# One weight through GpSimd's DMA queue, the next one held until the first copies of x are made, and a new split of the buffers

## The chip, the cores and the metric

The kernel runs on one core of one Trainium2 chip. The time is the device time of one execution in microseconds (us). The runs of the kernel before lie within 0.73 to 0.97 us in each of the four measurements of it (266.71 to 267.44 us in the first; 266.78 to 267.67, 266.73 to 267.50 and 266.60 to 267.57 in the others), that is 0.3 to 0.4% of 267, so everything here is near the resolution of the measurement: times are given as medians of several runs, with ratios and their 95% intervals, and the argument rests mainly on traces, where a single instruction can be placed to 0.01 us.

## The reference, cut to what matters

The input x has 2048 rows of 512. Two branches work on it and a gate mixes them:

```python
def _A_ref(x, wq, wk, wv, wo, beta):          # 32 heads of 16, 4 segments of 512 rows
    q, k, v = x @ wq, x @ wk, x @ wv          # ... split into heads and segments
    for s in range(4):
        # softmax attention inside the segment, plus a read of the memory M, z
        # that the segments before have left;  then M, z += phi(k)^T v, sum phi(k)
        ...
    return o @ wo
def _B_ref(x, W_gate, W_up, W_down):          # 512 -> 1792 -> 512
    return (relu(x @ W_gate) * (x @ W_up)) @ W_down
g = sigmoid((x * gate_w).sum(-1))
return g * a + (1 - g) * b
```

Each of wq, wk and wv is 512 x 512 bfloat16, 512 KB. The first segment of x is 512 KB as well. Nothing can be computed before x and wq are in, and K's projection needs wk.

## The kernel before: the parts that the change and the argument touch

The kernel is a list of operations with keys and estimated costs. A small scheduler inside it orders them for each engine when the program is built; on the chip the order is fixed. The start of the program is this (cuts marked with `...`):

```python
for _ in range(28):                            # warm-up of TensorE, on a tile of ones
    nc.tensor.matmul(g_dummy.t[:, 0:P], lhsT=zero[:, 0:P], rhs=zero[:, 0:P], start=True, stop=True)
...
for i in range(2):                             # i: column half of x, h: row half
    for eng, q, h in (("SP", nc.sync, 0), ("ACT", nc.scalar, 1)):
        ...  q.dma_start(out=xn[0].t[...], in_=x[...])          # 128 KB of x
    if i == 0:
        ...  q.dma_start(out=wq_sb[:, 0, cs], in_=A_wq[0:P, cs])  # wq chunk 0, 64 KB on SP, 64 KB on ACT
    else:
        ...  # wq chunk 1 (128 KB) on SP, chunks 2 and 3 (256 KB) on ACT
lw["wk"] = loadw("wk", wk_sb, A_wk, 0, D, 1)   # 512 KB, on SP
lw["wv"] = loadw("wv", wv_sb, A_wv, 0, D, 1)
...
first_x(0, None); first_x(1, None)             # TensorE transposes x, VectorE and ScalarE copy it to xT
for ci in range(NC):                           # q0.0 to q0.3: four matmuls of 512 columns each
    ...  nc.tensor.matmul(qS.t[:, c, :], lhsT=wq_sb[:, ci, ...], rhs=xT[0].t[:, ci, :], ...)
    if ci < 2: first_x(ci + 2, o_q0)
```

Then come K's projection (`wk_sb`, first seen as `G<-xT,wk_sb`), V's, and the long body: attention units (scores `S<-QT,K`, exponentials `E<-S`, masks, "PV" `G<-E,Vp`), mixed with the dense matmuls of the other branch. Buffers that the change touches:

```python
K2p = pool("K2", 6, [P, 8, 2, 64])
Ep = pool("E", 7, [P, 4, L])                   # the exponentials, until PV has read them
rgp = pool("rg", 3, [P, L]); osp = pool("os", 2, [P, D])
```

## Time and profile before

| | before |
|---|---|
| median of 4 runs | 266.94 us (266.71 to 267.44) |
| span of the profiled run | 265.7 us |
| TensorE busy | 256.3 us, 96% of the span |
| granted TensorE clock | 1.0 |
| first matmul of K's projection | 9.78 us |

The first lines are from the page of the kernel before: busy time by engine, and the head of the chain of work that ended last.

```profile
PE 256.3 (96%) x2795; PEld 114.5 (43%) x2832; DVE 182.5 (69%) x404; ACT 195.3 (73%) x191; POOL 188.4 (71%) x467
...
PE 95%; issue 2%; DMA 2%; SPq 0%; DVE 0%; DVEq 0%
```

TensorE is the bottleneck and has hardly a gap. What the chain has besides TensorE is 2% of DMA, and in order of time that is one piece at the start: 4.63 us from 2.27 us on, of a copy of wq. So the head is the place to look. This is TensorE's timeline there, in the kernel before (start, duration in us, engine, line, operation, count, and in brackets the idle time before it and what ended it):

```profile
1.11 3.13 PE L292 MATMUL G<-os 128*128 128x128 bf16 x28 [1.11 <-DVE mcole L269]
4.07 0.62 PE L390 MATMUL G<-ident,xn 128*128 128x128 bf16 x8
4.93 1.02 PE L411 MATMUL S<-xT,wq_sb 128*128 128x512 bf16 x4 [0.25 <-DVE xT L398]
6.34 0.48 PE L390 MATMUL G<-ident,xn 128*128 128x128 bf16 x4 [0.39 <-DMA xn<-in_A_x_dram]
6.96 1.04 PE L411 MATMUL S<-xT,wq_sb 128*128 128x512 bf16 x4
7.83 0.39 PE L390 MATMUL G<-ident,xn 128*128 128x128 bf16 x4
8.05 1.89 PE L411 MATMUL S<-xT,wq_sb 128*128 128x512 bf16 x7
9.78 2.75 PE L249 MATMUL G<-xT,wk_sb 128*128 128x512 bf16 x12
```

Read it as: 28 warm-up matmuls, transposes of x (`G<-ident,xn`), q0.0, a wait for the second pieces of x, transposes, q0.1, transposes, q0.2 and q0.3 (one record of eight is missing), then K. Four matmuls of 512 columns take 1.02 us when each starts 0.215 us after the one before. That number is used throughout below: **how long q0.0 takes tells the rate at which TensorE was running at that moment.**

The last piece is the page's list of DMA issues (median us from issue to landing):

```profile
wk_sb<-in_A_wk_dram SPq DMA_DIRECT2D x1, 512.0 KB, 5.9
xn<-in_A_x_dram ACTq DMA_DIRECT2D x2, 128.0 KB, 3.8
xn<-in_A_x_dram SPq DMA_DIRECT2D x2, 128.0 KB, 3.6
wq_sb<-in_A_wq_dram ACTq DMA_DIRECT2D x1, 256.0 KB, 5.0
wq_sb<-in_A_wq_dram SPq DMA_DIRECT2D x1, 128.0 KB, 4.6
```

wk was issued at 3.78 us and landed at 3.78 + 5.9 = 9.7 us, just when q0 was done.

### The profile page before, as it was taken

How to read it: one execution, taken by the hardware profiler on the slowest of the kernel's cores; microseconds unless marked ns; L12 is line 12 of the kernel's file. 1: busy time of each engine (PE TensorE's matmuls, PEld its weight loads, DVE VectorE, ACT ScalarE, POOL GpSimd, SP SyncE). 2: the span in 40 equal slices, each digit the busy share in tenths (PEclk: the TensorE clock that was granted, in tenths of full speed). 3: DMA queues.
4: the chain of work that ended last, by engine and by line, in shares of the span. 5: the costliest groups of instructions: out<-in, count | busy, mean ns of one | idle time of the engine just before them, and what ended most of it. 6: DMA issues, size and time to landing. Idle time of an engine off the chain costs nothing.

```text
span 265.7 us, 7041 instructions
## 1 busy us (share of the span) xinstructions
PE 256.3 (96%) x2795; PEld 114.5 (43%) x2832; DVE 182.5 (69%) x404; ACT 195.3 (73%) x191; POOL 188.4 (71%) x467
## 2 busy tenths in 40 slices
PE   7999999999999999999999999999999999999995
PEld 6434444444444444444444434344443444444444
DVE  1397888888975185998888837688985725466611
ACT  3498999899886658899896667898788566777010
POOL 8268888888559688798648988887878866537000
PEclk9999999999999999999999999999999999999999
DMA  6995991016310000000660010000000010000011
GB/s 171 309 268 145 333 241 25 2 38 78 103 23 23 22 20 22 0 2 0 131 109 3 23 42 21 2 0 2 0 2 4 0 42 20 23 2 0 2 41 39
DMA packets 27585, 15.54 MB, mean 58 GB/s; under 512 B 13600, under 2 KB 27552, under 8 KB 27552
## 3 DMA queue, kind: packets, MB, share of 16 engines
q1 hardware_dynamic: 26592, 14.50, 23.2%
q10 hardware_dynamic: 960, 0.59, 0.7%
q8 instruction: 22, 0.36, 0.6%
q14 instruction: 11, 0.09, 0.1%
HBM read 9.84 MB, written 2.10 MB: 45 GB/s over the span
## 4 chain that ended last, share of the span: by engine, by line
PE 95%; issue 2%; DMA 2%; SPq 0%; DVE 0%; DVEq 0%
PE G L249 74%; PE S L740 9%; PE G L852 7%; PE G L247 2%; DMA wq_sb<-in_A_wq_dram 2%; PE S L411 1%; PE G L613 1%; PE G L787 0%; SPq L317 0%; DVE os L702 0%; SPq L325 0%; PE G L390 0%; DVEq L702 0%
## 5 line engine op out<-in xcount | busy, mean ns | idle before, releaser
L754 ACT ACTIVATE E<-S 128x2048 bf16<-128x2048 f32 x72 | 135.1, 1876 | 32.1 <-PE S L740 29.4
L762 POOL TENSOR_SCALAR_AFFINE_SELECT E<-E 64x256 bf16<-64x256 bf16 x256 | 116.2, 454 | 39.2 <-ACT E L754 25.4
L249 PE MATMUL G<-xT,wu_sb 128*128 128x512 bf16 x210 | 57.1, 380 | 0.4 <-issue 0.2
L249 PE MATMUL G<-xT,wg_sb 128*128 128x512 bf16 x207 | 56.3, 380 | 1.1 <-issue 0.8
L665 DVE TENSOR_TENSOR hT<-G,rg 128x512 bf16<-128x512 f32 x56 | 38.2, 683 | 20.0 <-ACT rg L661 10.9
L249 PE MATMUL G<-wd_sb,hT 128*128 128x512 bf16 (+1 forms) x215 | 49.7, 366 | 1.3 <-issue 1.1
L887 DVE STREAM_TRANSPOSE T<-G 128x512 f32<-128x512 f32 x44 | 30.3, 702 | 13.0 <-PE G L852 8.2
L661 ACT ACTIVATE rg<-G 128x512 bf16<-128x512 f32 x56 | 32.7, 597 | 5.6 <-PE G L249 5.3
L249 PEld LDWEIGHTS <-wu_sb 128*128 128x128 bf16 x218 | 19.9, 98 | 24.8 <-issue 3.0
L249 PEld LDWEIGHTS <-hT 128*128 128x128 bf16 x226 | 20.5, 98 | 22.7 <-issue 3.0
L249 PEld LDWEIGHTS <-wg_sb 128*128 128x128 bf16 x218 | 19.4, 98 | 24.6 <-issue 4.1
L740 PE MATMUL S<-QT,K 32*128 32x192 bf16 (+7 forms) x512 | 28.6, 287 | 0.5
L740 PEld LDWEIGHTS <-K 32*128 32x128 bf16 x512 | 8.3, 92 | 30.2 <-issue 29.7
L702 DVE TENSOR_SCALAR os<-G,ngcol 128x512 bf16<-128x512 f32 (+1 forms) x8 | 5.5, 683 | 21.1 <-PE G L249 21.0
L852 PE MATMUL G<-E,Vp 64*32 64x128 bf16 (+7 forms) x512 | 19.0, 284 | 0.4 <-issue 0.4
L852 PE MATMUL G<-E,VS 64*32 64x128 bf16 (+7 forms) x512 | 18.4, 284 | 0.0
L599 POOL COPY VS<-Vp 64x256 bf16<-64x256 bf16 x32 | 12.9, 404 | 7.5 <-DVE Vp L517 6.0
L704 ACT ACTIVATE os<-G,ngcol 128x512 bf16<-128x512 f32 x9 | 6.2, 687 | 15.9 <-PE G L249 15.8
L249 PE MATMUL G<-wo_sb,oT 128*128 128x512 bf16 (+1 forms) x66 | 17.0, 367 | 0.3 <-issue 0.3
L907 DVE TENSOR_TENSOR O<-T,sm 128x256 bf16<-128x256 f32 x32 | 16.0, 529 | 0.3
L249 PE MATMUL G<-xT,wk_sb 128*128 128x512 bf16 x60 | 15.8, 380 | 0.3 <-issue 0.2
L481 POOL COPY R<-rcol 32x4 f32<-32x4 f32 x64 | 13.6, 212 | 3.0
(96 smaller groups left out, 295.5 us busy)
## 6 DMA issues: line engine op xcount, KB each, us to landing
out_dram<-os SPq DMA_DIRECT2D x15, 128.0 KB, 1.7
wd_sb<-in_B_W_down_dram SPq DMA_DIRECT2D x1, 1792.0 KB, 13.9
xn<-in_A_x_dram SPq DMA_DIRECT2D x3, 512.0 KB, 4.9
wg_sb<-in_B_W_gate_dram SPq DMA_DIRECT2D x2, 512.0 KB, 5.3
wu_sb<-in_B_W_up_dram SPq DMA_DIRECT2D x2, 512.0 KB, 6.6
wg_sb<-in_B_W_gate_dram SPq DMA_DIRECT2D x3, 256.0 KB, 6.7
wu_sb<-in_B_W_up_dram SPq DMA_DIRECT2D x3, 256.0 KB, 6.4
wk_sb<-in_A_wk_dram SPq DMA_DIRECT2D x1, 512.0 KB, 5.9
```

The lines of the kernel that those rows point to most:

```text
L249: nc.tensor.matmul(out_ap, lhsT=lhsT, rhs=rhs, start=start, stop=stop)
L481: nc.gpsimd.tensor_copy(R[s][32 * j:32 * j + 32, k, :], rcol[32 * k:32 * k + 32, cols])
L599: nc.gpsimd.tensor_copy(VS[s].t[64 * r:64 * r + 64, t, 0:H // 2 * HP].rearrange("p (h v) -> p h v", v=HP)[:, :, 0:DH], src[:, :, r, 0:DH])
L661: nc.scalar.activation(rg.t[:], g.t[:], ACT.Relu)
L665: nc.vector.tensor_tensor(h.t[:], u.t[:], rg.t[:], ALU.mult)
L704: nc.scalar.activation(ob.t[:, cs], g.t[:, 0:W], ACT.Copy, scale=ngcol[:, tt:tt + 1])
L740: nc.tensor.matmul(sp.t[:, j, off:off + w], lhsT=K2[s, cc].t[rows, kb, :, :].rearrange("p r k -> p (r k)"), rhs=QT[s, cc].t[rows, L - w:L] ...
L754: nc.scalar.activation(eb_.t[:], sp.t[:], ACT.Exp, scale=SCALE)
L762: nc.gpsimd.affine_select(out=v, in_=v, compare_op=ALU.is_ge, fill=0.0, base=0, pattern=[[0, 4], [1, 64]], channel_multiplier=-1)
L852: nc.tensor.matmul(gs[r].t[32 * j:32 * j + 32, L - w:L], lhsT=v, rhs=src.t[rows, j, off:off + w], start=(kb == 0), stop=(kb == 7), tile_po ...
L887: nc.vector.transpose(T.t[:].rearrange("p b e -> p (b e)"), g.t[:])
L907: nc.vector.tensor_tensor(O.t[:, :, r, :], T.t[:, :, 0:DH], sm.t[:, r, :, None].to_broadcast([P, 16, DH]), ALU.mult)
```

## The change

The intent: let x alone use SP's and ACT's queues, bring wq through GpSimd's queue at the same time, keep wk from competing with both until the first copy of x has been made, and use the space of some buffers for an eighth E. The hold on wk is a trick: VectorE writes one element of wk's tile after its first copies of x, so the load of wk must wait for that write. The diff, cut to its core:

```diff
-    K2p = pool("K2", 6, ...)
+    K2p = pool("K2", 5, ...)
-    Ep = pool("E", 7, [P, 4, L])
+    Ep = pool("E", 8, [P, 4, L])
-    rgp = pool("rg", 3, [P, L])
-    osp = pool("os", 2, [P, D])
+    osp = rgp = pool("os", 4, [P, D])
...
-        if i == 0:                     # wq on SP and ACT, between and after the pieces of x
-            ... (14 lines)
+    for n, (c0, c1) in enumerate(((0, 1), (1, 2), (2, 4))):
+        def f(e, c0=c0, c1=c1):
+            nc.gpsimd.dma_start(out=wq_sb[:, c0:c1, :], in_=A_wq[c0 * P:c1 * P, :].rearrange("(c p) n -> p c n", p=P))
+        o = op(f"wq{c0}", {"POOL": 1.0}, f, key=-110 + 15 * n, cls=0, land=131072 * (c1 - c0) / GBs)
...
     lw["wk"] = loadw("wk", wk_sb, A_wk, 0, D, 1)
+    o_wk0 = op("wk0", {"DVE": 0.08}, lambda e: nc.vector.memset(wk_sb[0:1, 0, 0:1], 0.0), key=-490, cls=0)
+    lw["wk"].deps.append((o_wk0, None))
...
+    o_wk0.deps.append((xc0[0][0], None))
...
-        (den and the memory update mz in one operation, with two PSUM buffers at once)
+        (mz an operation of its own, right behind den)
```

The rest of the diff makes the scheduler keep a valid order (the loads of later x segments are ordered behind wd, an operation may not start before its buffers have been given out).

More of the change, by code (lines that the diff above doesn't have):

```diff
@@ L59, in __init__, with op @@
         self.ops = []
-    def op(self, name, engs, emit, deps=(), key=0.0, cls=1, mode=None, alloc=(), uses=(), land=0.0, flex=False):
+    def op(self, name, engs, emit, deps=(), key=0.0, cls=1, mode=None, alloc=(), uses=(), land=0.0, flex=""):
         o = Op()
@@ L97, in run @@
                     t = max(free[e], o.ready)
-                    ok = True
+                    ok = all(b.idx is not None for b in o.uses[len(o.alloc):])
                     need = {}
@@ L119, in pk @@
                             k += -20.0 if mode == "R" else 4.0
-                        elif o.mode == "D" and mode == "C" and not o.flex:
+                        elif o.mode == "D" and mode == "C" and "C" not in o.flex:
                             k += 3.0
@@ L134, in run @@
             if e == "PE":
-                o.ran = "C" if o.flex and mode == "C" else o.mode
+                o.ran = mode if mode in o.flex else o.mode
                 if o.ran != mode:
@@ L213 @@
     hTp = pool("hT", 22, [P, L])
-    QTp, KTp, K2p = pool("QT", 6, [P, L]), pool("KT", 3, [P, L]), pool("K2", 6, [P, 8, 2, 64])
+    QTp, KTp, K2p = pool("QT", 6, [P, L]), pool("KT", 3, [P, L]), pool("K2", 5, [P, 8, 2, 64])
     pqp = pool("pq", 4, [P, L])
@@ L320 @@
                              uses=[] if (i, h) == (0, 0) else [xn[0]])
-        if i == 0:
-            for eng, q, h in (("SP", nc.sync, 0), ("ACT", nc.scalar, 1)):
-                def f(e, h=h, q=q):
-                    cs = slice(256 * h, 256 * h + 256)
-                    q.dma_start(out=wq_sb[:, 0, cs], in_=A_wq[0:P, cs])
-                lwq.setdefault(0, []).append(load(f"wq0{h}", f, 65536, -299.5, eng=eng))
-        else:
-            for c0, c1, eng, q in ((1, 2, "SP", nc.sync), (2, 4, "ACT", nc.scalar)):
-                def f(e, c0=c0, c1=c1, q=q):
-                    q.dma_start(out=wq_sb[:, c0:c1, :], in_=A_wq[c0 * P:c1 * P, :].rearrange("(c p) n -> p c n", p=P))
-                o = load(f"wq{c0}", f, 131072 * (c1 - c0), -298, eng=eng)
-                for ci in range(c0, c1):
-                    lwq[ci] = [o]
+    for n, (c0, c1) in enumerate(((0, 1), (1, 2), (2, 4))):
+        def f(e, c0=c0, c1=c1):
+            nc.gpsimd.dma_start(out=wq_sb[:, c0:c1, :], in_=A_wq[c0 * P:c1 * P, :].rearrange("(c p) n -> p c n", p=P))
+        o = op(f"wq{c0}", {"POOL": 1.0}, f, key=-110 + 15 * n, cls=0, land=131072 * (c1 - c0) / GBs)
+        for ci in range(c0, c1):
+            lwq[ci] = [o]
+    o_vones.deps.append((lwq[3][0], -1e9))
     def loadw(name, tile_, ap, c0, c1, key, eng="SP"):
@@ L422 @@
             lx[s] = xload(s, 10 + 60 * s)
+            for o in lx[s]:
+                o.deps.append((lwd, -1e9))
         xr[s] = [lx[s][0]]
@@ L509, in f @@
                     mm(g.t[:], lhs(ci), rhs(ci), ci == 0, ci == NC - 1)
-            prev = op(f"{name}/{i}", {"PE": 2 * MM}, f, deps=[(prev, 0.0)] if i else deps, key=dkey(2), mode="D", flex=True,
+            prev = op(f"{name}/{i}", {"PE": 2 * MM}, f, deps=[(prev, 0.0)] if i else deps, key=dkey(2), mode="D", flex="C",
                       alloc=[] if i else alloc, uses=uses + (alloc if i else []))
@@ L688, in dn @@
                           deps=[lwd, (prev, 0.0) if prev else None] + gate + [o_h[s, fb] for fb in range(p0, p1)],
-                          key=dkey((p1 - p0) / halves), mode="D", flex=True, alloc=[g] if p0 == 0 else [],
+                          key=dkey((p1 - p0) / halves), mode="D", flex="C", alloc=[g] if p0 == 0 else [],
                           uses=([] if p0 == 0 else [g]) + [hT[s, fb] for fb in range(p0, p1)])
@@ L697, in dn @@
                               deps=[lwo, (prev, 0.0)] + [o_oT[s, c] for c in (2 * i, 2 * i + 1)],
-                              key=dkey(2 / halves), mode="D", flex=True, uses=[g] + [oT[s, c] for c in (2 * i, 2 * i + 1)])
+                              key=dkey(2 / halves), mode="D", flex="C", uses=[g] + [oT[s, c] for c in (2 * i, 2 * i + 1)])
             def f(e, g=g, cs=cs):
@@ L788, in f @@
                                  start=True, stop=True, tile_position=(0, 32 * c))
-            if s < NSEG - 1:
-                mz_mm(s, gm)
-        gm, mds, mus = None, [], []
-        if s < NSEG - 1:
-            gm, mds, mus = Buf(G), mz_deps(s), [pK[s], Vp[s]]
-        a = op(f"den{s}", {"PE": MM + (0.5 if gm else 0.0)}, f,
-               deps=[o_pq[s, c] for c in range(NC)] + [o_m2[s - 1, c] for c in range(NC)] + mds,
-               key=k0, mode="C", alloc=[g] + ([gm] if gm else []), uses=[pq[s, c] for c in range(NC)] + mus)
-        rec_of[s, "den"] = a
-        if gm:
-            gate_mz.append((s, a, gm, k0))
+        mds = mz_deps(s) if s < NSEG - 1 else []
+        a = op(f"den{s}", {"PE": MM}, f,
+               deps=[o_pq[s, c] for c in range(NC)] + [o_m2[s - 1, c] for c in range(NC)] + mds,
+               key=k0, mode="C", alloc=[g], uses=[pq[s, c] for c in range(NC)])
+        rec_of[s, "den"] = rec_of[s, "mz"] = a
+        if mds:
+            gm = Buf(G)
+            rec_of[s, "mz"] = am = op(f"mz{s}", {"PE": 0.5}, lambda e: mz_mm(s, gm), deps=[(a, 0.0)], key=k0 - 20, mode="C",
+                                      alloc=[gm], uses=[pK[s], Vp[s]])
+            gate_mz.append((s, am, gm, k0))
         T = Buf(Tp)
@@ L866, in rest @@
             a = op(f"rec{s}{c}", {"PE": MM}, f, deps=[o_pq[s, c], o_m2[s - 1, c], (prev_pv, 0.0)],
-                   key=k0 + 3.6 * PU / 5, mode="D", flex=True, alloc=[g], uses=[pq[s, c]])
+                   key=k0 + 3.6 * PU / 5, mode="D", flex="C", alloc=[g], uses=[pq[s, c]])
             recs.append((a, g))
```

## The prediction

> **What bounds the kernel now.** TensorE: the page gives it 96% busy over a span of 265.7 us at granted clock 1.0, and the chain of waits that ended last is 95% TensorE, 2% DMA. By stretches, TensorE idles only 4.0 us between 30 and 250 us, in pieces of about 0.2 us[...], and 3.6 us at the tail. So only the head is left for a different order of loads.
>
> The head, from the timeline: x's first halves are transposed at 4.07 us, q0.0 runs 4.93 to 5.95, the second x pieces release the next transposes at 6.34, q0.1 starts at 6.96 on the landing of wq's second chunk (in the chain, a 4.63 us DMA ending at 6.90), q0.2 at 8.05, and K's projection at 9.7 exactly when wk lands. wk was issued at 3.78 us, because SP waited 1.0 us for the first x piece, and took 5.9 us. From 4 us on the DMA share is 0.9 to 1.1 (270 to 330 GB/s)[...].
>
> **What the change does.**
> 1. Four wq copies leave SP and ACT, where each issue took 0.44 to 0.53 us. x's second pieces go out at 1.3 instead of 1.8 us with no wq piece ahead of them; I expect them landed near 5.3 instead of 6.3.
> 2. wq comes in three copies from GpSimd. [...] wq's chunks landed near 4.5, 6 and 7.2 us.
> 3. GpSimd's memsets of V's tiles (4.08 + 2.17 us) end near 10.5 instead of 7.5; the first V copy is at 13.95: no harm.
> 4. wk waits for VectorE's first two x copies and a one-element memset: issued near 5.0 instead of 3.78, but after x, so it takes 4.3 instead of 5.9 us and lands near 9.3. wv is issued 1 us later but lands hardly later[...]; it is first used at 12.4.
> 5. Eighth E buffer, shared rg/os, five K2, mz split from den: only some 14 TensorE groups of 570 change place, around the start of segment 1; tiling changes stay 171. ScalarE waited 1.7 us for E's readers in all, off the chain. Worth about 0.1 us.
>
> **On the critical path.** q0 should end near 8.9 instead of 9.94 us, but K then waits for wk until 9.3. So K starts 0.4 to 0.5 us sooner, which passes to the end as TensorE is full from there. With 0.1 us from the body: 267.1 - 0.6 = 266.5 us.
>
> **Predicted 266.5 us, 8 in 10 between 265.4 and 267.6. Faster by over 2%: 0.01; within 2%: 0.98; slower: 0.01.**
>
> **What would show it.** Right: x's second pieces landed by 5.5 us; first K matmul at 9.0 to 9.5, waiting for wk; q0.1 waiting for wq, not x; TensorE idle between 30 and 250 us still 4 us. Wrong: K's first matmul at or after 9.8 (the hold or GpSimd's issue costs too much), or before 8.8 (wk lands sooner), or a body shorter by over 0.5 us (a buffer did matter).
>
> **What would make it wrong.** GpSimd's copies costing far more than 1 us each, so that wq lands last; wv or the first gate weights pushed past their use (12.4 and 16.1 us); a fixed cost of a third queue at start or end, which this profile cannot show.

## More of the kernel before

Of the single run of e1, its trace is used and its time (267.11 us) is not compared.

## The result, and the profile after

| | before | after |
|---|---|---|
| first measurement, median (runs) | 266.94 us (4) | 266.91 us (4) |
| ratio, 95% interval | | 0.9993 [0.9973, 1.0012] |
| second measurement (e2), median (runs) | 267.09 us (11) | 266.63 us (5) |
| ratio, 95% interval | | 0.998 [0.9967, 0.9994] |
| span of the first profiled run | 265.7 us | 265.3 us |
| first matmul of K's projection | 9.78 us | 9.60 us |

A ratio is the mean time of one kernel's fast runs over that of the other's of the same rounds, so it is not quite the ratio of the medians. By the ratios the change is worth 0.2 us (0.07%, an interval that includes nothing) and 0.5 us (0.2%): the second near the 0.6 that was predicted, the first well below it, both far within 2%.

The same views of the kernel after:

```profile
PE 257.0 (97%) x2808; PEld 115.9 (44%) x2844; DVE 183.8 (69%) x407; ACT 193.9 (73%) x189; POOL 191.0 (72%) x470
...
PE 97%; issue 2%; DVE 0%; ACT 0%; DVEq 0%
```

The DMA has left the chain: it is TensorE now from the first warm-up matmul to the end. Its timeline of the head, in the kernel after:

```profile
1.12 3.17 PE L291 MATMUL G<-os 128*128 128x128 bf16 x28 [1.12 <-DVE mcole L268]
4.08 1.06 PE L385 MATMUL G<-ident,xn 128*128 128x128 bf16 x8
5.18 1.54 PE L406 MATMUL S<-xT,wq_sb 128*128 128x512 bf16 x4
6.56 0.39 PE L385 MATMUL G<-ident,xn 128*128 128x128 bf16 x4
6.79 1.03 PE L406 MATMUL S<-xT,wq_sb 128*128 128x512 bf16 x4
7.65 0.39 PE L385 MATMUL G<-ident,xn 128*128 128x128 bf16 x4
7.87 1.89 PE L406 MATMUL S<-xT,wq_sb 128*128 128x512 bf16 x7
9.60 2.75 PE L248 MATMUL G<-xT,wk_sb 128*128 128x512 bf16 x12
```

and the landings:

```profile
wk_sb<-in_A_wk_dram SPq DMA_DIRECT2D x1, 512.0 KB, 4.0
...
xn<-in_A_x_dram ACTq DMA_DIRECT2D x2, 128.0 KB, 3.1
xn<-in_A_x_dram SPq DMA_DIRECT2D x2, 128.0 KB, 2.8
wq_sb<-in_A_wq_dram POOLq DMA_DIRECT2D x2, 128.0 KB, 3.2
wq_sb<-in_A_wq_dram POOLq DMA_DIRECT2D x1, 256.0 KB, 3.3
```

x and wk arrive sooner after their issue than before: x in 2.8 to 3.1 instead of 3.6 to 3.8 us, wk in 4.0 instead of 5.9. (wq's later pieces take 3.2 to 3.3 instead of 4.6 to 5.0 us; its first one does not gain, it had come in two halves in 2.7 and 2.9 us.) No wait for a DMA is left in TensorE's head in this trace. Yet K starts only 0.18 us sooner. The reason stands in two lines: the eight transposes took 1.06 us instead of 0.62, and q0.0 took 1.54 us instead of 1.02. The same matmuls ran at half the rate until about 6.3 us. The page's granted clock says 1.0 in both kernels, so it does not show this.

The theory to test, a guess of the author at this point, is that TensorE starts at half its full rate and that the moment at which it gets the full one falls differently in each execution; how far the traces agree is said under "All the traces together". If it holds, the single pair of traces compares an early moment (before) with a late one (after), and says too little of the change.

After K's start the program is nearly rigid. On the chain that ended last, the first PV group starts 23.03 us after K in the kernel before (32.81 - 9.78) and 23.03 us after it in the kernel after (32.63 - 9.60). In all fourteen traces of this document the first PV matmul comes 22.90 to 22.97 us after K. From K's start to the end of the span it is 255.3 to 255.9 us in thirteen of them, and 256.5 in e4. So what K's start gains is kept, but the rest of the program varies by up to 0.6 us from trace to trace, which is as much as the change gains.

### The profile page after: what moved, and what is told of

Same layout as the page of the kernel before. It is cut to its first block, busy times and chain, and to the rows that moved or that the text cites. A ratio compares the mean times of both kernels' runs of the same rounds, so it can differ in the third digit from the quotient of the medians.

```text
span 265.3 us, 7048 instructions
## 1 busy us (share of the span) xinstructions
PE 257.0 (97%) x2808; PEld 115.9 (44%) x2844; DVE 183.8 (69%) x407; ACT 193.9 (73%) x189; POOL 191.0 (72%) x470
## 4 chain that ended last, share of the span: by engine, by line
PE 97%; issue 2%; DVE 0%; ACT 0%; DVEq 0%
PE G L248 74%; PE S L738 9%; PE G L849 7%; PE G L246 3%; PE S L406 2%; PE G L291 1%; PE G L611 1%; PE G L785 0%; PE G L385 0%; DVE os L700 0%; ACT xT L395 0%; DVE os L253 0%; DVE mcole L268 0%; DVEq L700 0%; DVE mcol L267 0%
## 5 line engine op out<-in xcount | busy, mean ns | idle before, releaser
L663 DVE TENSOR_TENSOR hT<-G,os 128x512 bf16<-128x512 f32 x56 | 38.2, 684 | 19.7 <-ACT os L659 10.7
L248 PE MATMUL G<-wd_sb,hT 128*128 128x512 bf16 (+1 forms) x212 | 48.9, 365 | 1.1 <-issue 1.0
L659 ACT ACTIVATE os<-G 128x512 bf16<-128x512 f32 x56 | 32.7, 597 | 6.1 <-PE G L248 5.3
L700 DVE TENSOR_SCALAR os<-G,ngcol 128x512 bf16<-128x512 f32 (+1 forms) x10 | 7.0, 697 | 19.4 <-PE G L248 19.3
L702 ACT ACTIVATE os<-G,ngcol 128x512 bf16<-128x512 f32 x7 | 4.8, 687 | 15.0 <-PE G L248 15.0
```

What stands on the lines that cost most here:

```text
L248: nc.tensor.matmul(out_ap, lhsT=lhsT, rhs=rhs, start=start, stop=stop)
L659: nc.scalar.activation(rg.t[:], g.t[:], ACT.Relu)
L663: nc.vector.tensor_tensor(h.t[:], u.t[:], rg.t[:], ALU.mult)
```

## The experiments

Theory A: TensorE's clock comes up at a moment that differs from execution to execution; the change turns a head bound by loads into one bound by TensorE's own work; so its gain depends on that moment. Theory B: 9.60 us is what the new order gives, whatever the execution. A further question is which part does it: wq's new queue (theory: free queues for x), the hold on wk, or the buffers.

Three measurements were made, of four kernels each, every one with its own runs of the kernel before on the same chip (11 runs each, median 267.09, 267.17 and 267.19 us).

### e1 and e2: both kernels once more, unchanged

> The kernel before, unchanged, for a second trace. Theory A (the clock decides): in the first pair of traces the kernel before had its TensorE at the full matmul rate (0.11 us spacing of 128-column matmuls falling to about 0.055) by about 4.2 us, the changed one only at about 6.6 us, although TensorE's program up to there is the same. If that moment is free-running, it falls elsewhere in this trace than at 4.2 us[...], and K's projection starts later than 9.78 us if it falls late (up to about 10.3). Theory B (the change's own doing): the rate doubles at 4.2 us again, K starts at 9.7 to 9.8 us. The rest of the program is fixed: PV of the first unit starts 23.0 us after K's start in either theory (32.81 - 9.78).

> The changed kernel, unchanged, for a second trace and a tighter ratio. Theory A: the moment of full rate moves; if it comes by 5 us, K starts at about 9.3 to 9.4 us (then on wk's landing, which took until 9.3 us) instead of 9.60. Theory B: full rate again at 6.6 us, K at 9.60. Ratio to before: A and B both 0.997 to 1.000, as the traces gave 0.4 us of 266.

Measured: e1 one run for its trace. e2 266.63 us, ratio 0.998 [0.9967, 0.9994]. In e1, the kernel before, TensorE's timeline has these lines:

```profile
4.07 1.06 PE L390 MATMUL G<-ident,xn 128*128 128x128 bf16 x8
5.17 1.58 PE L411 MATMUL S<-xT,wq_sb 128*128 128x512 bf16 x4
...
9.89 2.76 PE L249 MATMUL G<-xT,wk_sb 128*128 128x512 bf16 x12
```

So the kernel before, too, can have its transposes at 1.06 us and q0.0 at 1.58: the rate is not the change's doing. And K starts at 9.89, only 0.11 us later than in the trace with the early clock, because the loads were late anyway: now wk's weight load waits 0.6 us for wk's landing. In e2, the changed kernel, q0.0 took 1.36 us and K started at 9.42, not at 9.60:

```profile
5.18 1.36 PE L406 MATMUL S<-xT,wq_sb 128*128 128x512 bf16 x4
...
9.42 2.75 PE L248 MATMUL G<-xT,wk_sb 128*128 128x512 bf16 x12
```

Theory B falls: the same kernel gives two starts.

### e3 and e4: the loads alone, and the rest alone

e3 is the kernel before with the new loads (wq on GpSimd, wk held); TensorE's order is then exactly that of before. e4 is the kernel after with the old loads; TensorE's order is that of after.

```diff
 # e3, from the kernel before                    # e4, from the kernel after
-wq on SP and ACT                               -wq on GpSimd, in three copies
+wq on GpSimd, in three copies                  +wq on SP and ACT
+wk0 memset, wk waits for it                    -wk0 memset
```

> The kernel before with only wq moved to GpSimd's queue and wk held (the scheduler's order of TensorE is then exactly that of before). If the loads are what gained at the head: K starts at 9.3 to 9.7 us, ratio 0.998 to 0.9995. The 0.35 us pause of TensorE near 46 us before the last PV matmul of a unit, which was 0.15 us in the changed kernel, tells whether that belongs to the buffers: it should be 0.35 here if the buffers and the order did it, and anything if it is chance.

> The changed kernel with the loads of before: eight E, shared rg/os, five K2, mz split from den. K should start as in the kernel before (9.78 at an early full rate, later at a late one). If the buffers gained: the pause near 46 us is 0.15 us and the ratio 0.999. If they are worth nothing: pause as in before or any, ratio 1.000 within 0.001. The split of mz from den seemed to cost 0.08 us between 75 and 92 us; that should be here as well.

Measured: e3 266.60 us, ratio 0.9979 [0.9967, 0.9991]; q0.0 took 1.19 us, K started at 9.31, and its weight load had waited for wk (us in total, times, longest):

```profile
5.18 1.19 PE L407 MATMUL S<-xT,wq_sb 128*128 128x512 bf16 x4
...
9.31 2.76 PE L249 MATMUL G<-xT,wk_sb 128*128 128x512 bf16 x12
...
PEld L249 <- DMA wk_sb<-in_A_wk_dram: 0.4, 1, 0.4
```

e4 267.61 us, ratio 1.0021 [1.0006, 1.0035]; q0.0 1.02 us (an early clock), K at 9.91 after a wait of 0.29 us for wk.

The loads alone give all of the gain. The rest gives none. With the old loads K does not start before 9.78 even at an early clock. What made e4 slower than before is not the head alone: its trace shows a longer pause inside a PV group near 46 us, at the same instruction as in the kernel before. The lines are the last PV matmul of that group in before and in e4:

```profile
46.41 0.19 PE L852 MATMUL G<-E,Vp 64*32 64x64 bf16 x1 [0.35 <-issue]
```

```profile
46.74 0.19 PE L852 MATMUL G<-E,Vp 64*32 64x64 bf16 x1 [0.62 <-issue]
```

It waited for nothing that the profile shows. The changed kernel has 0.15 us there in its first trace and 0.21 in e2; e1 and e3 have no pause listed there. The eight E buffers do not remove it.

### e5: the hold taken away

The one-element memset goes to another tile, so all instructions keep their order and only the wait of wk's load is gone:

```diff
-    o_wk0 = op("wk0", {"DVE": 0.08}, lambda e: nc.vector.memset(wk_sb[0:1, 0, 0:1], 0.0), ...)
+    o_wk0 = op("wk0", {"DVE": 0.08}, lambda e: nc.vector.memset(nohold[0:1, 0:1], 0.0), ...)
```

> The changed kernel with the hold on wk taken away (the one-element memset goes to another tile, so the order of all instructions stays). wk is then issued right behind x's pieces at about 1.8 us instead of 5.3 and is in flight beside wq. Theory A (TensorE's own clock and work set K's start in the new order, wk was not in the way): K starts at the end of q0 as before, 9.3 to 9.6 us, ratio as the changed kernel, 0.998. Theory C (the hold is what makes the new order work, because wk's 512 KB share the 16 engines with wq): wq's chunks land later, q0.1 or q0.2 wait for them by 0.5 us or more, K starts at 9.8 or later, ratio 1.000. If the hold costs instead: K starts before 9.2.

Measured: 271.55 us, ratio 1.0162 [1.0143, 1.0181]. Theory C is right, and by far more than expected. TensorE's timeline in e5:

```profile
4.03 0.61 PE L386 MATMUL G<-ident,xn 128*128 128x128 bf16 x8
5.43 1.04 PE L407 MATMUL S<-xT,wq_sb 128*128 128x512 bf16 x4 [0.79 <-DMA wq_sb<-in_A_wq_dram]
6.30 0.39 PE L386 MATMUL G<-ident,xn 128*128 128x128 bf16 x4
8.48 1.04 PE L407 MATMUL S<-xT,wq_sb 128*128 128x512 bf16 x4 [1.80 <-DMA wq_sb<-in_A_wq_dram]
9.36 0.39 PE L386 MATMUL G<-ident,xn 128*128 128x128 bf16 x4
11.16 3.17 PE L407 MATMUL S<-xT,wq_sb 128*128 128x512 bf16 x7 [1.42 <-DMA wq_sb<-in_A_wq_dram]
```

K starts only here:

```profile
14.38 2.75 PE L249 MATMUL G<-xT,wk_sb 128*128 128x512 bf16 x12
```

wk and wv, issued at 1.83 and 2.33 us, now go beside wq, and all three pieces of wq come late. (In the kernel after, SP issued wk at 5.31 us and wv behind it at 5.72, so the hold had kept back wv as well. e5 frees both: wk landed at 8.8 and wv at 10.4 us, before the last piece of wq at 11.1, and which of the two costs how much is not shown.) The last one needs this long:

```profile
wq_sb<-in_A_wq_dram POOLq DMA_DIRECT2D x1, 256.0 KB, 7.9
```

instead of 3.3 us. The waits of TensorE for wq are 0.79 + 1.80 + 1.42 = 4.0 us. On top of that the last eight q0 matmuls ran at half rate (0.43 us apart). By stretches (length, busy time and count of TensorE, its weight loads, VectorE, ScalarE and GpSimd, then granted clock, DMA share, GB/s), this is e5 from 10 to 12 us:

```profile
10.00:12.00 2.00, 0.84 (x3) 0.29 (x4) 0.00 (x0) 0.17 (x1) 1.22 (x6) 0.70 1.18 316
```

The granted clock is 0.70 here: within the third of the waits TensorE lost its full clock (the clock record kept in the trace has it at half from 10.79 to 14.20 us). That the waits were the cause is the author's reading and is not shown. K starts at 14.38 us, 4.96 us later than in e2, and the time is 4.9 us longer than e2's (271.55 - 266.63). The DMA engines had not moved fewer bytes: their share is 1.18 in that stretch, with 316 GB/s (in the kernel after: 0.82 and 228 GB/s). They moved the wrong ones first.

### e6 and e7: one warm-up matmul instead of 28, in both kernels

```diff
-        for _ in range(28):
+        for _ in range(1):
```

> The changed kernel with 1 warm-up matmul instead of 28. Theory A: TensorE is then at half rate (weight loads of 0.15 instead of 0.10 us, 512-column matmuls 0.43 instead of 0.216 us apart)[...], so K starts at 10.5 to 12 us, and the kernel is 1 to 2.5 us slower (1.004 to 1.009). If the warm-up matmuls do nothing: 266.6 us as the changed kernel.

> The kernel before with 1 warm-up matmul. Theory A: at half rate the head is bound by TensorE in both kernels, so the order of loads is worth little here: K starts within 0.3 us of what the changed kernel without warm-up shows for the same moment of full rate, and the two times differ by less than the 0.5 us between the two with warm-up. If loads bind nevertheless, the difference stays 0.5 us or grows.

Measured: e6 267.71 us, ratio 1.002 [1.0006, 1.0034]; e7 267.25 us, ratio 1.0016 [0.9996, 1.0037], both against the kernel before with its 28. TensorE's q0.0 and q0.1 in e6:

```profile
4.87 1.89 PE L406 MATMUL S<-xT,wq_sb 128*128 128x512 bf16 x4 [0.42 <-ACT xT L395]
...
6.97 1.91 PE L406 MATMUL S<-xT,wq_sb 128*128 128x512 bf16 x4
```

1.9 us for four is the half rate, to the end of q0.1; K started at 10.80. In e7's trace the full rate came earlier (q0.0 1.86, q0.1 1.27 us) and K started at 9.82. At a slow clock the changed kernel's advantage is not seen any more: 1.002 against 1.0016, where with warm-up it was 0.998 against 1. That fits theory A, by which the order of loads pays only if TensorE could run faster than the loads allow, but it does not show it. The two traces have their full rate at different moments, so K's starts in them can't be compared as the expectation wanted, and intervals of this width do not show equality to better than 0.3%, more than the 0.2% in question.

### e8: the rest alone, again

> e4 once more, for a second trace: old loads, new buffers and mz split. e4 was 0.5 us slower than before (ratio 1.0021), of which its trace showed 0.35 to 0.6 us in two pauses of TensorE (0.62 us near 46 us before the last PV matmul of a unit; about 0.35 us near 80 us among down-projection matmuls) that the other traces have at the same places with 0 to 0.35 us. If the pauses are chance: ratio here between 0.999 and 1.001, pauses of another size. If the rest costs with the old loads: ratio 1.002 again and the same pauses.

Measured: 267.29 us, ratio 1.0006 [0.9993, 1.0018]. q0.0 took 1.02 us and K started at 9.80 (after wk). The cost of 0.5 us that e4 showed did not come again, and its trace lists no pause near 46 us. Of the buffers and the split of mz one can say that they gave nothing in two measurements; whether they cost 0.1 us is not settled.

### e9: the hold alone

The kernel before with only the hold on wk; wq stays on SP and ACT.

```diff
+    o_wk0 = op("wk0", {"DVE": 0.08}, lambda e: nc.vector.memset(wk_sb[0:1, 0, 0:1], 0.0), ...)
+    lw["wk"].deps.append((o_wk0, None))
```

> The kernel before with the hold on wk alone (wq stays on SP's and ACT's queues). In the kernel before wk's issue waited until 3.78 us anyway[...], so wk was already half held. If the hold is the whole gain, K starts at 9.3 to 9.6 us and the ratio is 0.998. If the gain needs wq off the queues of x: wk is issued at about 4.9 instead of 3.78, lands no earlier (9.7 to 10.3 us), K starts there, ratio 1.000 to 1.002.

Measured: 266.89 us, ratio 0.9993 [0.9977, 1.0009]. wk was issued at 5.3 us and landed 4.7 us later, at 10.0; K started at 10.01, in a trace with a late clock (q0.0 1.87 us), where q0 itself ended at 10.0 as well (8.28 + 8 x 0.215). So wk's landing comes later than with the old loads (9.7 to 9.9 us in before, e8, e1 and e4), and K does not start sooner in this trace; the interval of the time allows a gain of up to 0.2%. So neither part works well alone: the new queue without the hold costs 4.4 us against before (with the rest of the change in it, as e5 is built), the hold without the new queue is not told apart from zero.

### e10 to e12: the loads alone again, and two tries to do better

e11 takes 20 warm-up matmuls instead of 28, since x had landed at 3.40 us in e6 while 28 of them keep TensorE until 4.08. e12 does the same and sends wq's first chunk on ACT's queue between the two pieces of x. Both, like e10, are built on e3.

```diff
 # e11 and e12
-        for _ in range(28):
+        for _ in range(20):
 # e12 also
+            lwq[0] = [load("wq0", f, 131072, -299.5, eng="ACT")]   # after x's first piece on ACT
```

> The loads alone (e3) once more, as the partner of the next two on the same chip and for one more moment of full rate: K at 9.3 if full rate comes by 6.2 us or earlier, up to 9.6 at 6.6; ratio 0.998.

> The loads alone, with 20 warm-up matmuls instead of 28. Without them x had landed by 3.40 us, while 28 half-rate matmuls hold TensorE until 4.08: 20 end at about 3.3, so the transposes and the x copies come 0.6 us sooner, wk's issue with them (4.7 instead of 5.3, landing near 8.7). q0.0 then waits for wq's first chunk (landed at 4.86 to 5.12). If TensorE's clock rises as before: K starts 0.2 to 0.4 us sooner than in e10, ratio 0.9965 to 0.9975. [...]

> As e11, and wq's first chunk goes out on ACT's queue between the two x pieces (issued at 1.3 us, landing near 4.1 instead of 4.9), the other two stay with GpSimd and leave 0.7 us sooner. If q0.0 was held by wq's first chunk in e11: q0.0 starts at 4.4 to 4.6 us, K at 8.8 to 9.3, ratio 0.995 to 0.997. If the second x pieces on ACT land later by that chunk (5.5 instead of 4.6) it costs nothing as long as q0.0 is running until then.

Measured: e10 266.78 us, ratio 0.9984 [0.997, 0.9998]. e11 267.68 us, ratio 1.0019 [0.9995, 1.0043]. e12 266.74 us, ratio 0.9979 [0.9965, 0.9993]. The lines of e10 are those of the new loads with the early clock that the first trace of the change had missed:

```profile
5.15 1.02 PE L407 MATMUL S<-xT,wq_sb 128*128 128x512 bf16 x4 [0.25 <-DVE wk_sb L336]
...
9.24 2.76 PE L249 MATMUL G<-xT,wk_sb 128*128 128x512 bf16 x12
...
PEld L249 <- DMA wk_sb<-in_A_wk_dram: 0.5, 1, 0.5
```

(The wait before q0.0 is put down to VectorE's last semaphore; what ended it was wq's first chunk, which landed at 5.07.) K at 9.24. q0 was finished by then, by about 0.2 us (the last eight matmuls start at 7.32 and take 8 x 0.215 us, to 9.04), and wk's landing at 9.2 was the limit, as the prediction had it.

e11 shows the other side. x's transposes began at 3.59, half a microsecond sooner, but TensorE stayed at half rate through q0.1:

```profile
5.09 1.89 PE L407 MATMUL S<-xT,wq_sb 128*128 128x512 bf16 x4 [0.41 <-ACT xT L396]
...
7.20 1.91 PE L407 MATMUL S<-xT,wq_sb 128*128 128x512 bf16 x4
```

and K started at 11.20. Its runs fall into two groups (266.81 to 267.07, and 268.29 to 268.72 us), with 1.2 us between them; that fits a clock that comes up earlier in one group than in the other, though only the slower group has a trace (full clock from 9.60 us on). e12 has q0.0 at 4.80 and K at 9.39, after a wait of 0.27 us for wk. It has the same 20 warm-up matmuls, full clock from 5.34 us on, and no slow group in its six runs; so that the shorter warm-up made e11 slow is likely, but not shown. It is no faster than e10 beyond the noise. No version was found that beats the loads alone; of the tried ones the loads alone (e3, e10), the whole change (e2) and e12 are the fastest, each about 0.2% below before.

### All the traces together

Here is the start of K against the duration of q0.0, for every trace with the 28 warm-up matmuls and the hold or the old loads. A longer q0.0 means that the clock came up later. The moment itself is on record too: each run's packed trace keeps a list of the clock changes, of which the profile's views print only means. Its first entry is the rise to the full clock, and what lies before that entry is counted as full in the means; that is why they say 1.0. The third column has that moment, in us from the span's start.

| loads | q0.0 took | full clock from | K started | trace |
|---|---|---|---|---|
| old | 1.02 us | 4.07 us | 9.78 us | before |
| old | 1.02 us | 3.96 us | 9.80 us | e8 |
| old | 1.02 us | 3.98 us | 9.91 us | e4 |
| old | 1.58 us | 6.33 us | 9.89 us | e1 |
| old, and wk held | 1.87 us | 7.12 us | 10.01 us | e9 |
| new | 1.02 us | 4.51 us | 9.24 us | e10 |
| new | 1.19 us | 5.55 us | 9.31 us | e3 |
| new | 1.36 us | 5.90 us | 9.42 us | e2 |
| new | 1.54 us | 6.27 us | 9.60 us | after |

So the first part of theory A is shown by the record itself: the same kernel had its full clock from 4.07 us (before) and from 6.33 us (e1), and the matmuls start twice as often from these moments on (every 0.056 instead of 0.107 us for 128 columns). With the same 28 warm-up matmuls the moment lies between 3.96 us (e8) and 7.12 us (e9). The record also has the length of some stretches: 262.83 us at the full clock in before, 259.41 in after, and in e5 6.83 us full, then 3.41 us half; these are 77, 76, 2 and 1 times 3.413 us. That the gain depends on this moment is shown by the starts of K in the table, not by the times, which vary by as much.

With the old loads K starts at 9.8 to 9.9 us at an early clock and at one that comes more than 2 us later alike: the loads are the limit and hide the slow start. (At the still later clock of e9 TensorE's own work reaches 10.0 us too.) With the new loads K's start rises with q0.0, step by step. In e10 and e3 wk's landing is still the limit (9.19 and 9.26 us; TensorE would have been ready at 9.05 and 9.25), in e2 and after TensorE's clock is (ready at 9.42 and 9.60, wk landed at 9.33 and 9.34). The gain is about 0.6 us at an early clock (9.83, the mean of the first three, less 9.24) and 0.3 us at a late one (9.89 - 9.60).

## Why the prediction was right

The forecast was 266.5 us, within 265.4 to 267.6; measured were 266.91 and 266.63 us. The range also holds the old time, 266.94, so the number alone shows little: a change that did nothing would have met it too. In the first measurement the gain was 0.2 us with an interval that includes nothing, in the second 0.5 of the 0.6 that were forecast. What was foreseen is the mechanism at the head. Point by point:

- **"What bounds the kernel now."** Right. TensorE and, at the head, the loads: the chain lost its 2% of DMA with the change, and the rest stayed where it was.
- **x's second pieces landed by 5.5 us.** Right: issued by about 1.3 us, landed within 3.3 us at most, so by 4.6.
- **wq's three copies.** Each issue took GpSimd 0.57 to 0.74 us; the scheduler of the change is told 1.0 (`{"POOL": 1.0}`), which was the author's estimate. The first chunk came later than forecast (4.9 to 5.1 us; e2's weight load waits for it until 5.12, the forecast had 4.5), the others sooner (5.3 to 5.6 and 6.4, against 6 and 7.2).
- **wk near 9.3.** Right: issued at 5.31, landed 4.0 us later.
- **K's first matmul between 9.0 and 9.5, 0.4 to 0.5 us sooner.** Missed by 0.1 in the first trace (9.60), right in e2 (9.42), e3 (9.31) and e10 (9.24). What was predicted to hold it, wk's landing, holds it only when TensorE's clock comes up early enough (e10 and, just so, e3); otherwise TensorE itself does. In the prediction's own terms, q0 should have ended near 8.9 instead of 9.94; it ended at 9.2 (e10), 9.4 (e3), 9.6 (e2) and 9.8 us (after). The prediction took the rate of TensorE in the one trace of before as given and had no term for its clock. That term is up to 0.4 us here, as large as the gain.
- **q0.1 waiting for wq.** Wrong: in the first trace of the change TensorE waited for nothing in the head.
- **The body worth 0.1 us.** Not shown. The rest alone was 1.0021 and 1.0006 of before, and the whole change (e2, 266.63) was no faster than the loads alone in the same measurement (e3, 266.60).
- **TensorE's idle time between 30 and 250 us stays near 4 us.** By stretches 4.1 us before and 3.8 after in the first pair, but nearly all of it is no idle time: these two traces lack 37 and 36 matmul records. In the complete traces of the same two kernels it is 0.0 (e1) and 0.2 us (e2). So the "pieces of about 0.2 us" of the prediction were missing records. What is real is the pause near 46 us, whose size changes by 0.6 us from trace to trace; neither says anything of the change.
- **A fixed cost of a third queue.** None seen: in the profiled runs time less span is 1.7 us in both kernels (267.44 - 265.7, 266.97 - 265.3).
- **Seen too small: the hold.** It was costed as a delay of wk by 1.2 us, paid back by a quicker transfer. e5 shows what it really prevents: 4.9 us.

What stays open: why the pause near 46 us comes and goes; why in e5 wq's last 256 KB on GpSimd's queue, issued at about 3.2 us, landed at 11.1, after the 1 MB of wk and wv on SP's queue (10.4); and whether the buffers cost a tenth of a microsecond.

## What to carry to other kernels

Loads that share the DMA engines should be issued in the order in which they are needed, and if they sit on different queues, something must enforce that order: here the same loads cost 4.9 us more when the later weights were free to run beside the earlier one (e5 against e2). When a head is freed from its loads, look at once at what bounds it next; here that was TensorE's clock, which came up between 3.96 and 7.12 us with 28 warm-up matmuls, so that one pair of traces showed 0.18 us of a gain that nine traces together put at 0.3 to 0.6. Read the rate of the matmuls themselves before comparing two traces of a start, and don't cut a warm-up to start real work sooner without measuring it several times: with 20 matmuls (2.3 us) instead of 28 (3.2 us) the transposes started 0.5 us sooner, but K at 11.20 (e11) and 9.39 us (e12, with wq's first chunk on ACT's queue), against 9.24 with 28 (e10).
